# A Fourier filter and a gated layer in one kernel: the order and the padding of the constant tiles

## The chip, the cores and the metric

One core of one Trainium2 chip runs the whole program. The metric is device time in microseconds of that core. The kernel before was timed in three runs; the profile is one more, profiled, execution.

## The reference

Two steps follow each other. The first filters each of 8 sequences (3008 steps, 256 channels) in the frequency domain; the second sends the 24064 resulting tokens through a layer 256 to 2048 to 256 with a rational function between.

```python
X = np.fft.rfft(x, axis=1)
Y = X * (filt_r + 1j * filt_i)[None, :, :]
x2 = np.fft.irfft(Y, n=x.shape[1], axis=1).reshape(B * S, D)

h = x2 @ w_in
P = a[0] + a[1] * h + a[2] * h * h + a[3] * h ** 3
Q = 1.0 + abs(b[0]) * abs(h) + abs(b[1]) * h * h
out = (P / (Q + 1e-06)) @ w_out
```

## The kernel before

The Fourier transform of 3008 = 64 x 47 points is done as matrix products, in fp32. Stage 1 (L290) multiplies the input `xin` by the matrix `a1_sb`, a view of `small_sb` (L298), and sends the result through a scratch buffer in HBM (`scr`). Stage 2 multiplies by the first of three 128 x 128 matrices in `mats_sb` (L346), by the filter with signs from `sgn_sb` (L331, L353, L354, L365), by the second or third matrix (L379, L381), and stores to a second scratch buffer. Stage 3 (L408) multiplies tiles `tl` of that buffer by `e_sb`, the other view of `small_sb` (L424), and splits the result into a high and a low part, `xh` and `xl`, in the type fp32r.

The layer then runs in 752 units: 47 tiles of 512 tokens, 16 slices of 128 hidden rows each. A unit makes six matmuls of 128 x 128 by 128 x 512 from `wi_sb` and `xh`, `xl` into a PSUM bank (L457, L458, L460). ScalarE forms squares, an absolute value and a reciprocal root of it (L465 to L487), GpSimd a scaled term and a product (L497, L516), VectorE the numerator and the high and low part of the result, `hi` and `lo` (L502, L511, L519, L525). Six more matmuls with `wo_sb` add into two output banks (L534 to L536). The scalars of these steps are columns of `cf_sb`, computed once at the start from `ab_sb` and `abs_sb` by some 50 small steps (L138 to L187), and four of them are loaded into registers of ScalarE (L190).

The weights come as 64-bit numbers; 16 pieces are decoded into `wi_sb` and `wo_sb` (high and low parts, L210 to L246), 12 of them while batch 0 is transformed. Batches 1 to 7 are transformed in between the units. TensorE, ScalarE, VectorE and GpSimd run in the order in which the program is written; the DMA queue of SyncE does so in the head, and is ordered by the planner afterwards.

All tiles in SBUF come from pools that are laid out one behind the other: constants (L114 to L125, in this order: small_sb, mats_sb, sgn_sb, ab_sb, wi_sb, wo_sb, abs_sb, cf_sb, flag_sb), then `conv`, `mlp` and `x`. Each tile takes its bytes per partition, rounded up to 32. The first byte of the constants is 16512 = 129 x 128.

Of the kernel before, what the change touches and what calls it, by code (L numbers as in the profile page):

```python
# [9 lines left out]
F32 = mybir.dt.float32  # L10
F32R = mybir.dt.float32r
I32 = mybir.dt.int32
# [13 lines left out]
K2 = 24  # L26
R1 = 96
C = 256
G = 94
DFF = 2048  # L30
LAG = 4
RATES = 0.6, 0.38
# [26 lines left out]
def shape_constants():  # L59
    n2 = np.arange(N2)  # L60
    k2 = np.arange(K2)
    th = 2 * np.pi * np.outer(n2, k2) / N2
    a1 = np.zeros((48, 2, K2, 2, 2))
    for h in range(2):
        a1[:N2, h, :, 0, h] = np.cos(th)
        a1[:N2, h, :, 1, h] = -np.sin(th)
    a1 = a1.reshape(R1, R1)

    ph = 2 * np.pi * np.outer(np.arange(N1), np.arange(N1)) / N1
    co, si = np.cos(ph), np.sin(ph)  # L70
    fwd = np.block([[co, -si], [si, co]])
    inv = np.block([[co, si], [-si, co]])

    e = np.zeros((K2, 2, 2, 2, N2))
    w = np.where(k2 == 0, 1.0, 2.0) / S
    for h in range(2):
        e[:, 0, h, h, :] = w[:, None] * np.cos(th.T)
        e[:, 1, h, h, :] = -w[:, None] * np.sin(th.T)
    e = e.reshape(R1, G)

    k = (N2 * np.arange(N1)[:, None] + N1 * k2[None, :]) % S
    sgn = np.where(k > S // 2, -1.0, 1.0)
    sgn[(k == 0) | (k == S // 2)] = 0.0
    sgn = np.concatenate([sgn, -sgn], 0)
    mats = np.zeros((128, 3, 128))
    mats[:, 0], mats[:, 1], mats[:, 2] = fwd, inv, np.concatenate([inv[64:], inv[:64]])
    small = np.zeros((R1, R1 + G))
    small[:, :R1], small[:, R1:] = a1, e
    f = lambda v: np.ascontiguousarray(v, dtype=np.float32)
    return f(mats), f(small), f(sgn)  # L90

# [10 lines left out]
def conv_moe(ctx: ExitStack, tc: tile.TileContext, xp, fr, fi, w_in, w_out, ab, mats, small, sgn, outT):  # L102
# [3 lines left out]
    consts = ctx.enter_context(tc.tile_pool(name="consts", bufs=1))  # L106
# [4 lines left out]
    ps = ctx.enter_context(tc.tile_pool(name="ps", bufs=1, space=PSUM))  # L111
    pso = ctx.enter_context(tc.tile_pool(name="pso", bufs=1, space=PSUM))

    small_sb = consts.tile([R1, R1 + G], F32, name="small_sb")  # L114
    a1_sb, e_sb = small_sb[:, :R1], small_sb[:, R1:]
    mats_sb = consts.tile([128, 3, 128], F32, name="mats_sb")
    sgn_sb = consts.tile([128, K2], F32, name="sgn_sb")
    ab_sb = consts.tile([128, 12], F32, name="ab_sb")

    wi_sb = consts.tile([128, 4, 2, 2, TT], F32R, name="wi_sb")  # L120
    wo_sb = consts.tile([128, 8, 2, TT], F32R, name="wo_sb")
    xh = xl = None
    abs_sb = consts.tile([128, 12], F32, name="abs_sb")
    cf_sb = consts.tile([128, 24], F32, name="cf_sb")
    flag_sb = consts.tile([128, 1], I32, name="flag_sb")  # L125

    v = nc.vector
    ts, tt, stt = v.tensor_scalar, v.tensor_tensor, v.scalar_tensor_tensor
# [279 lines left out]
    def stage3(k):  # L408
# [11 lines left out]
        for cc in range(2):  # L420
            yield 1.1
            bank, pt = banks.tile(f"x_{k}_{cc}")
            for i in range(g1 - g0):
                nc.tensor.matmul(  # L424
                    pt[:, i * G : i * G + G], tl[:, i, cc * 128 : cc * 128 + 128], e_sb, start=True, stop=True
                )
            yield

            t0, t1 = g0 * G, g1 * G
            cut = min(t1, (t0 // RX + 1) * RX)  # L430
# [129 lines left out]
    def run(gen):  # L560
        for _ in gen:
            pass
# [85 lines left out]
    def pipeline(squares):  # L648
# [10 lines left out]
        for i in range(n + LAG + 2 * OG):  # L659
# [14 lines left out]
            if i < 16:  # L674
# [4 lines left out]
                while dec.done < i // 4 * 4 + 3:  # L679
                    dec.load()  # L680
                    dec.step()
            if f == 0 and xgen and T * (t + 1) > chunks[xk - 1][0] * G:
                run(xgen)
# [134 lines left out]
```

## Time and profile before

| | us |
|---|---|
| median of 3 runs | 2585.64 (2584.13 to 2586.91) |
| the profiled execution | 2588.73 |
| its span, from first to last instruction | 2586.1 |

| engine | busy us | share |
|---|---|---|
| PE (matmul) | 2526.4 | 98% |
| DVE (VectorE) | 2269.5 | 88% |
| ACT (ScalarE) | 2198.9 | 85% |
| POOL (GpSimd) | 1856.3 | 72% |

PE is the time in which a matmul was under way; neighbouring matmuls overlap, so their mean durations add up to more than the span. PEld is the loading of weights, which runs beside the matmuls. The mean granted clock of TensorE was 0.989 of full speed. In the rows, L12 is line 12 of the kernel.

### The profile page before, as it was taken

How to read it: one execution, taken by the hardware profiler on the slowest of the kernel's cores; microseconds unless marked ns; L12 is line 12 of the kernel's file. 1: busy time of each engine (PE TensorE's matmuls, PEld its weight loads, DVE VectorE, ACT ScalarE, POOL GpSimd, SP SyncE). 2: the span in 40 equal slices, each digit the busy share in tenths (PEclk: the TensorE clock that was granted, in tenths of full speed). 3: DMA queues.
4: the chain of work that ended last, by engine and by line, in shares of the span. 5: the costliest groups of instructions: out<-in, count | busy, mean ns of one | idle time of the engine just before them, and what ended most of it. 6: DMA issues, size and time to landing. Idle time of an engine off the chain costs nothing.

```text
span 2586.1 us, 35887 instructions
## 1 busy us (share of the span) xinstructions
PE 2526.4 (98%) x10712; PEld 1936.0 (75%) x10712; DVE 2269.5 (88%) x3549; ACT 2198.9 (85%) x4170; POOL 1856.3 (72%) x1984
## 2 busy tenths in 40 slices
PE   4799999999999999999999999999999999999998
PEld 1467777777777777777777777777777778888886
DVE  5689988999889998899888998899988999899998
ACT  4588889888988889888888889888888889999997
POOL 3468876788668876778657886688757787677676
PEclk8799999999999999999999999999999999999999
DMA  8653331332223231232223332233323210000000
GB/s 248 181 139 104 100 113 51 107 93 86 71 75 100 81 95 53 84 109 83 74 61 105 86 93 71 67 101 88 87 61 94 82 37 28 25 25 17 25 9 18
DMA packets 102813, 208.76 MB, mean 81 GB/s; under 512 B 8752, under 2 KB 58512, under 8 KB 102608
## 3 DMA queue, kind: packets, MB, share of 16 engines
q1 hardware_dynamic: 99568, 199.79, 26.5%
q10 hardware_dynamic: 3040, 6.58, 1.0%
q8 instruction: 87, 1.43, 0.2%
q14 instruction: 118, 0.97, 0.1%
HBM read 131.36 MB, written 74.97 MB: 80 GB/s over the span
## 4 chain that ended last, share of the span: by engine, by line
PE 95%; DVE 2%; DMA 2%; ACT 1%; issue 0%; ACTq 0%; SPq 0%; DVEq 0%
PE o L534 13%; PE o L535 13%; PE o L536 13%; PE h_u L458 13%; PE h_u L460 13%; PE h_u L457 13%; PE x L424 4%; PE s L298 4%; PE y L346 3%; PE z L379 3%; DMA scr<-s1e 1%; DMA xin<-xp 0%; ACT s1e L263 0%; DMA ab_sb<-ab 0%; DVE hi_u L511 0%
## 5 line engine op out<-in xcount | busy, mean ns | idle before, releaser
L516 POOL TENSOR_TENSOR q_u<-q_u,hi_u 128x512 f32<-128x512 f32 x752 | 974.6, 1296 | 526.8 <-DVE hi_u L511 509.3
L534 PE MATMUL o<-hi_u,wo_sb 128*128 128x512 f32 x1504 | 705.6, 469 | 0.0
L465 ACT ACTIVATE q_u<-h_u 128x512 f32<-128x512 f32 x752 | 450.5, 599 | 243.3 <-PE h_u L460 175.2
L511 DVE SCALAR_TENSOR_TENSOR hi_u<-h_u,cf_sb,a_u 128x512 fp32r<-128x512 f32 x752 | 559.9, 745 | 76.4 <-ACT a_u L487 68.0
L519 DVE SCALAR_TENSOR_TENSOR h_u<-h_u,cf_sb,q_u 128x512 f32<-128x512 f32 x752 | 565.4, 752 | 54.1 <-POOL q_u L516 53.7
L457 PE MATMUL h_u<-xh,wi_sb 128*128 128x512 f32 x1504 | 604.3, 402 | 3.1 <-DVE xl L435 1.9
L458 PE MATMUL h_u<-xl,wi_sb 128*128 128x512 f32 x1504 | 596.9, 397 | 0.0
L535 PE MATMUL o<-lo_u,wo_sb 128*128 128x512 f32 x1504 | 594.3, 395 | 1.4 <-DVE lo_u L525 1.4
L536 PE MATMUL o<-hi_u,wo_sb 128*128 128x512 f32 x1504 | 594.2, 395 | 0.0
L497 POOL TENSOR_SCALAR q_u<-q_u,cf_sb 128x512 f32<-128x512 f32 x752 | 584.0, 777 | 3.6 <-ACT a_u L482 3.6
L502 DVE SCALAR_TENSOR_TENSOR h_u<-w_u,cf_sb,h_u 128x512 f32<-128x512 f32 x752 | 561.5, 747 | 4.3 <-ACT w_u L472 4.3
L525 DVE TENSOR_TENSOR lo_u<-h_u,a_u 128x512 fp32r<-128x512 f32 x752 | 514.3, 684 | 0.1
L482 ACT ACTIVATE a_u<-q_u 128x512 f32<-128x512 f32 x752 | 475.3, 632 | 0.1
L460 PE MATMUL h_u<-xh,wi_sb 128*128 128x512 f32 x1504 | 473.8, 396 | 0.0
L487 ACT ACTIVATE a_u<-a_u 128x512 f32<-128x512 f32 x752 | 470.3, 625 | 0.0
L478 ACT ACTIVATE q_u<-q_u 128x512 f32<-128x512 f32 x752 | 469.4, 624 | 0.0
L472 ACT ACTIVATE w_u<-h_u 128x512 f32<-128x512 f32 x752 | 443.9, 590 | 0.0
L534 PEld LDWEIGHTS o<-hi_u,wo_sb 128*128 128x128 f32 x1504 | 282.8, 188 | 117.2 <-issue 63.3
L535 PEld LDWEIGHTS o<-lo_u,wo_sb 128*128 128x128 f32 x1504 | 283.0, 188 | 116.7 <-issue 60.3
L457 PEld LDWEIGHTS h_u<-xh,wi_sb 128*128 128x128 f32 x1504 | 283.4, 188 | 77.9 <-issue 3.6
L458 PEld LDWEIGHTS h_u<-xl,wi_sb 128*128 128x128 f32 x1504 | 283.5, 188 | 73.2 <-issue 4.4
L460 PEld LDWEIGHTS h_u<-xh,wi_sb 128*128 128x128 f32 x1504 | 283.6, 189 | 69.1
(96 smaller groups left out, 1888.9 us busy)
## 6 DMA issues: line engine op xcount, KB each, us to landing
xin<-xp SPq DMA_DIRECT2D x64, 384.0 KB, 3.8
scr<-s1e SPq DMA_DIRECT2D x64, 384.0 KB, 4.1
xin<-scr SPq DMA_DIRECT2D x48, 512.0 KB, 4.9
scr<-ev SPq DMA_DIRECT2D x48, 512.0 KB, 4.8
outT<-oe SPq DMA_DIRECT2D x47, 512.0 KB, 3.1
f<-fr SPq DMA_DIRECT2D x87, 256.0 KB, 4.1
f<-fi SPq DMA_DIRECT2D x87, 256.0 KB, 3.9
tl<-scr SPq DMA_DIRECT2D x44, 480.0 KB, 4.0
```

The source lines that it names most:

```text
L457: nc.tensor.matmul(o, w_in_part(0, f, cc), xh[:, cc, ts], start=cc == 0, stop=False)
L458: nc.tensor.matmul(o, w_in_part(0, f, cc), xl[:, cc, ts], start=False, stop=False)
L460: nc.tensor.matmul(o, w_in_part(1, f, cc), xh[:, cc, ts], start=False, stop=cc == 1)
L497: nc.gpsimd.tensor_scalar(out=self.q, in0=self.q, scalar1=AIK, scalar2=SGN, op0=ALU.mult, op1=ALU.add)
L502: v.scalar_tensor_tensor(out=H, in0=w, scalar=PK, in1=H, op0=ALU.add, op1=ALU.mult)
L511: nc.vector.scalar_tensor_tensor(out=self.hi, in0=self.H, scalar=self.p0, in1=self.a, op0=ALU.add, op1=ALU.mult)
L516: nc.gpsimd.tensor_tensor(out=self.q, in0=self.q, in1=self.hi.bitcast(F32), op=ALU.mult)
L519: nc.vector.scalar_tensor_tensor(out=self.H, in0=self.H, scalar=self.p0, in1=self.q, op0=ALU.add, op1=ALU.subtract)
L525: nc.vector.tensor_tensor(out=self.lo, in0=self.H, in1=self.a, op=ALU.mult)
L534: nc.tensor.matmul(o, w_out_part(0, f, dd), self.hi, start=f == 0, stop=False)
L535: nc.tensor.matmul(o, w_out_part(0, f, dd), self.lo, start=False, stop=False)
L536: nc.tensor.matmul(o, w_out_part(1, f, dd), self.hi, start=False, stop=f == 15)
```

## The change

The constants are allocated in another order and with other sizes. `wi_sb` and `wo_sb` come first, then `mats_sb`, then `small_sb`, whose second matrix gets 96 columns in place of 94 (the last two zero; `e_sb` is still 94 columns wide). The five small constants become columns of one tile `words` of 128 words: `sgn_sb` from column 0, `ab_sb` from 32, `abs_sb` from 64, `cf_sb` from 96, and the flag in column 120. No instruction is added or taken away; the array `small` that the program is given is 96 x 192 and not 96 x 190.

```diff
+GE = 96
...
-    small = np.zeros((R1, R1 + G))
-    small[:, :R1], small[:, R1:] = a1, e
+    small = np.zeros((R1, R1 + GE))
+    small[:, :R1], small[:, R1 : R1 + G] = a1, e
...
-    small_sb = consts.tile([R1, R1 + G], F32, name="small_sb")
-    a1_sb, e_sb = small_sb[:, :R1], small_sb[:, R1:]
-    mats_sb = consts.tile([128, 3, 128], F32, name="mats_sb")
-    sgn_sb = consts.tile([128, K2], F32, name="sgn_sb")
-    ab_sb = consts.tile([128, 12], F32, name="ab_sb")
...
     wi_sb = consts.tile([128, 4, 2, 2, TT], F32R, name="wi_sb")
     wo_sb = consts.tile([128, 8, 2, TT], F32R, name="wo_sb")
     xh = xl = None
-    abs_sb = consts.tile([128, 12], F32, name="abs_sb")
-    cf_sb = consts.tile([128, 24], F32, name="cf_sb")
-    flag_sb = consts.tile([128, 1], I32, name="flag_sb")
+    mats_sb = consts.tile([128, 3, 128], F32, name="mats_sb")
+    small_sb = consts.tile([R1, R1 + GE], F32, name="small_sb")
+    a1_sb, e_sb = small_sb[:, :R1], small_sb[:, R1 : R1 + G]
+    words = consts.tile([128, 128], F32, name="words_sb")
+    sgn_sb, ab_sb, abs_sb, cf_sb = words[:, :K2], words[:, 32:44], words[:, 64:76], words[:, 96:120]
+    flag_sb = words[:, 120:121].bitcast(I32)
```

## Rows read from the trace of the kernel before

**Rows 1.** The page: span, busy us and share, the chain's share by engine.
```profile
span 2586.1 us, 35887 instructions
...
PE 2526.4 (98%) x10712; PEld 1936.0 (75%) x10712; DVE 2269.5 (88%) x3549; ACT 2198.9 (85%) x4170; POOL 1856.3 (72%) x1984
...
PE 95%; DVE 2%; DMA 2%; ACT 1%; issue 0%; ACTq 0%; SPq 0%; DVEq 0%
```

**Rows 2.** The page's groups: line, count | busy us, mean ns | idle before; one of six.
```profile
L460 PE MATMUL h_u<-xh,wi_sb 128*128 128x512 f32 x1504 | 473.8, 396 | 0.0
```

**Rows 3.** Timeline of PE in the tail: start us, us, line; twelve steps apart.
```profile
2570.98 0.39 PE L534 MATMUL o<-hi_u,wo_sb 128*128 128x512 f32 x1
...
2573.78 0.39 PE L534 MATMUL o<-hi_u,wo_sb 128*128 128x512 f32 x1
```

**Rows 4.** Windows: length, busy us (count) by engine, PEclk, DMA share, GB/s.
```profile
101.00:106.00 5.00, 5.00 (x12) 3.60 (x12) 0.97 (x3) 2.38 (x7) 2.56 (x2) 0.50 1.00 266
2470.00:2570.00 100.00, 100.00 (x430) 80.17 (x429) 97.08 (x149) 94.81 (x182) 73.93 (x73) 1.00 0.03 11
0.00:105.00 105.00, 62.58 (x136) 27.99 (x137) 63.21 (x134) 44.12 (x71) 41.73 (x52) 0.83 0.83 237
```

**Rows 5.** The chain in order of time, steady stretch: start us, us, what.
```profile
1035.55 0.86 PE s L298 x2
1039.20 1.09 PE x L424 x10
```

**Rows 6.** Timeline of PE in the head, first units: start us, us, line.
```profile
102.64 0.63 PE L457 MATMUL h_u<-xh,wi_sb 128*128 128x512 f32 x1
103.07 0.63 PE L458 MATMUL h_u<-xl,wi_sb 128*128 128x512 f32 x1
```

**Rows 7.** Tiles mats_sb and wi_sb, weight loads: ns min/median/max, first and last start.
```profile
L346 PEld LDWEIGHTS y<-xin,mats_sb x192: 186/188/337, 52.3 to 2123.5; 128*128 128x128 f32 x192
...
L457 PEld LDWEIGHTS h_u<-xh,wi_sb x1504: 186/188/338, 101.3 to 2568.4; 128*128 128x128 f32 x188
```

**Rows 8.** Groups of the first 200 us, decoding on DVE: busy us, mean ns.
```profile
L234 DVE SCALAR_TENSOR_TENSOR dp<-raw,dp 128x512 int32<-128x512 int32 x16 | 11.1, 696 | 0.6
...
L238 DVE SCALAR_TENSOR_TENSOR dq<-raw,dp 128x512 f32<-128x512 uint32 x12 | 8.2, 686 | 0.4
```

**Rows 9.** Timeline of DVE in a steady unit: start us, us, line.
```profile
1500.28 0.68 DVE L525 TENSOR_TENSOR lo_u<-h_u,a_u 128x512 fp32r<-128x512 f32 x1
...
1502.85 0.68 DVE L525 TENSOR_TENSOR lo_u<-h_u,a_u 128x512 fp32r<-128x512 f32 x1
```

**Rows 10.** The chain in order of time, head: start us, us, what.
```profile
0.73 5.24 DMA ab_sb<-ab
...
6.84 1.28 ACT L138
...
15.54 0.23 DVE cf_sb L187
...
16.15 2.05 ACT s1e L263 x4
...
100.96 9.91 DMA xin<-xp
```

**Rows 11.** DMA issues by line: queue, count, KB each, us to landing.
```profile
xin<-scr SPq DMA_DIRECT2D x48, 512.0 KB, 4.9
...
outT<-oe SPq DMA_DIRECT2D x47, 512.0 KB, 3.1
...
small_sb<-small ACTq DMA_DIRECT2D x1, 71.2 KB, 7.0
```

**Rows 12.** Tiles sgn_sb and cf_sb: ns min/median/max, first to last start us; landing us.
```profile
L615 ACTq DMA_DIRECT2D sgn_sb<-sgn x1: 444/444/444, 6.4 to 6.4; - x1
...
DMA to landing us min/median/max: 8.3/8.3/8.3
...
L190 ACTq TENSOR_LOAD <-cf_sb x4: 275/281/473, 12.3 to 15.8; - x4
```

## The prediction

> **What bounds the kernel now.** I read the page from the top: the span, the busy line and the chain. PE is busy 98% of 2586.1 us, 95% of the chain that ended last runs through it, and nothing else has more than 2% of the chain [rows 1]. The groups of the page say what PE does: six lines (L457, L458, L460, L534 to L536) with 1504 matmuls each, 9024 in all, on fp32r operands of 512 columns [rows 2]. Their mean durations overlap, so they are no price. The price is the spacing of starts. In the tail, twelve steps on PE from 2570.98 take 2.80 us, 233.3 ns each [rows 3]. A window of 100 us ahead of it holds 430 matmuls, 232.6 ns each, at clock 1.00 with PE busy throughout [rows 4]. So 9024 x 233.3 ns = 2105 us of the span is this one stream. The convolution's fp32 passes come from the chain in order of time: two L298 passes take 0.86 us (430 ns each), ten L424 pieces 1.09 us (109 ns each) [rows 5]. By the loops, with each product in two passes, there are 256 of L298, 192 of L346, 216 of L379 and L381, and 1024 of L424; taken at these prices that is (256 + 192 + 216) x 0.430 + 1024 x 0.109 = 397 us. Together 2502 of 2586 us; the other 84 us lie in the head, the first 105 us, where PE is busy 62.58 us, the clock is 0.83 and the DMA share 0.83 [rows 4].
>
> One thing in these rows matters for a change of addresses. A 430 ns pass is two sweeps of 512 columns, 215 ns each. The fp32r matmul has one sweep and takes 233.3 ns: an excess of 18.3 ns that is there 9024 times, 165 us in all. [...]
>
> **The change part by part.** No instruction is added or taken away, no wait is written, no queue is reordered. What moves is addresses. The allocator rounds each tile up to 32 bytes, and the constants begin at byte 16512, 129 x 128. Before: small_sb 768, mats_sb 1536, sgn_sb 96 and ab_sb 64 bytes put wi_sb and wo_sb at 32 past a multiple of 128; abs_sb, cf_sb and flag_sb (64 + 96 + 32) put every tile of the pools behind (xin, ev, filters, tl, oe, a, w, q, hi, lo, xh, xl) at 96 past one. small_sb and mats_sb were at 0. After: 32768 + 32768 + 1536 + 768 + 512 bytes, all at 0, and the pools move up by 160 bytes.
>
> Weights, 32 to 0: the trace has weight loads from both places. L346 loads from mats_sb (at 0), median 188 ns; L457 from wi_sb (at 32), median 188 ns [rows 7]. Price 0, and the load is not what PE waits for, since it fits in each 233 ns.
>
> Moving operands, 96 to 0: no row shows an fp32r stream from a start at 0, so I bound it. The nearest rows are the 430 ns passes of L298, whose moving operand xin also lay at 96 and which run without the excess [rows 5]; that speaks against the address. The lower end is the excess gone, 9024 x 18.3 = -165 us. The upper end: weights and moving operand were 64 bytes apart modulo 128 and now start alike; if their reads get in each other's way by 1 ns more per matmul, that is +9 us. I take 0, by the row of L298. [...]
>
> VectorE, ScalarE, GpSimd: the same 512 elements, written to PSUM (L234, 696 ns) or to a tile at 96 (L238, 686 ns), cost the same on VectorE [rows 8]. Price 0; if a few ns went, PE would hide it, for VectorE needs 2.57 us per unit of four such steps (1500.28 to 1502.85) [rows 9] and PE 12 x 233.3 = 2.80. The cover is 0.23 us per unit: it also says what is late next if PE got faster.
>
> DMA: the rows of 4096 bytes in SBUF start at other addresses. On the chain this counts in the head alone; its DMA pieces in the chain are 5.24, 6.02, 4.61, 9.61, 6.15, 3.85, 3.17, 2.34 and 9.91 us, together 51 us (first and longest in [rows 10]). Even a tenth of it, either way, would be 5 us; I take 0, as the same 512 KB lands in 3.1 us from oe and 4.9 us into xin, both at 96: the load on the engines sets it, not the place [rows 11]. small_sb grows from 71.2 to 72 KB, 1% of a landing of 7.0 us, 0.1 us.
>
> Scalars: sgn, ab, abs, cf and the flag now share one tile. Columns, engines and order stay; price 0 as long as the waits stay by columns (rival 2).
>
> Sum: 0 + 0 + 0 + 0.1 against the profiled 2588.7 us (span 2586.1 and 2.6 around it). The median of the runs shown is 3.1 us lower, 2585.6; I forecast 2585.
>
> **The rivals.** 1: the start address is what holds the fp32r stream. For it: the excess is the same 18.3 ns in all six lines, and all of them have the same addresses modulo 128. Against it: the fp32 passes from 96, and weight loads that don't care. Whole: 2585.6 - 165 = 2421; VectorE with 2.57 us per unit would then lie just under PE with 12 x 215 = 2.58, so some of it would go back. In part: each ns of the 18.3 is 9.0 us; three ns give 2559. [...]
>
> 2: slower, by the shared tile. If waits are held per tile and not per column, the first ScalarE step (L138, at 6.84 [rows 10]) and all small VectorE steps behind it wait for the sign table, issued at 6.4 and landed 8.3 us later, at 14.7 [rows 12]. Then the chain of small steps that ends with L187 at 15.54 and lets the first evacuation start at 16.15 comes 7.8 us later [rows 10], with stage 1 queued behind it on ScalarE: 2585.6 + 7.8 = 2593. It decides from 5.2 us on. Against it: ScalarE's first register load from cf_sb starts at 12.3, while VectorE still writes other columns of cf_sb until 15.54 [rows 10, 12]. So the wait goes by columns, not by the tile.
>
> 3: slower, by reads of weights and moving operand that now begin alike, as priced above: from 0.6 ns per matmul on it would show, 1 ns gives 2595. Nothing in the trace speaks for it.
>
> **How the numbers follow.** A measurement of this kernel can tell 0.2%, 5.2 us. No change: 0.62. Rival 1 whole 0.08, in part 0.16; rival 2 0.05; rival 3 0.09. So faster 0.24, same 0.62, slower 0.14. The range from 2556 to 2598 holds the first, about two thirds of the partial gains (up to 3.3 ns per matmul), rival 2, and rival 3 up to 1.4 ns; whole recovery is left out.
>
> **What would show it.** In the changed kernel: the spacing of matmul starts in the tail, 233.3 ns again or less, decides between the forecast and rivals 1 and 3; in the matmul-only window the count of 430 in 100 us says the same. Weight loads at 188 ns and L238 at 686 ns would show that the other readers and writers don't care. L138 at 6.8 us and the first evacuation at 16.2 us show that the shared tile adds no wait. The forecast is wrong if the spacing moves by over 0.6 ns, or if the first unit's matmul starts over 5 us from 101.3 [rows 7].

## The result

The changed kernel takes 2542.89 us (median of 4 runs, 2542.57 to 2545.82) against 2586.27 us for the kernel before (median of 4 runs): a ratio of 0.9833, 95% interval 0.9816 to 0.9850, 43 us less. The prediction, 2585 us and no change, was wrong, and the time lies 13 us under the range.

The page of the changed kernel, the lines that answer to [rows 1]: span, busy us and share, the chain's share by engine.

```profile
span 2543.2 us, 35887 instructions
...
PE 2479.4 (97%) x10712; PEld 1934.2 (76%) x10712; DVE 2264.1 (89%) x3549; ACT 2197.0 (86%) x4170; POOL 1850.8 (73%) x1984
...
PE 93%; DVE 2%; DMA 2%; ACT 1%; issue 0%; SPq 0%; ACTq 0%; DVEq 0%
```

The same instructions in the same number; nearly all of the busy time that went is PE's, 47 us; VectorE, ScalarE and GpSimd lost 6 us or less each. The timeline of PE in the tail, beside [rows 3], shows how (start us, us, line; twelve steps from the first to the last):

```profile
2528.14 0.39 PE L534 MATMUL o<-hi_u,wo_sb 128*128 128x512 f32 x1
2528.37 0.39 PE L535 MATMUL o<-lo_u,wo_sb 128*128 128x512 f32 x1
...
2530.86 0.39 PE L534 MATMUL o<-hi_u,wo_sb 128*128 128x512 f32 x1
```

2.72 us for twelve steps are 226.7 ns each, where it was 233.3. Over the whole layer after 200 us, the mean of the differences between neighbouring matmul starts (those over 260 ns, where PE does something else between, left out) fell from 233.3 to 228.1 ns. Over all 9024 matmuls that is 9024 x 5.2 = 47 us. In this profiled execution the first unit starts 5 us later than in [rows 7] (106.4 against 101.3 us), which leaves 42 us, and the span fell by 42.9. A second profiled execution of the changed kernel (after_again, below) starts its first unit at 102.5 us, so the later start is not shown to come from the change.

Windows of the changed kernel (length, busy us (count) for PE, PEld, DVE, ACT and POOL, granted clock, DMA share, GB/s), beside [rows 4]:

```profile
2430.00:2530.00 100.00, 100.00 (x443) 82.85 (x442) 99.15 (x153) 97.51 (x187) 75.98 (x75) 1.00 0.03 11
0.00:105.00 105.00, 59.30 (x123) 25.23 (x124) 62.35 (x131) 42.22 (x66) 39.04 (x50) 0.82 0.81 228
```

The window holds 443 matmuls in 100 us where there were 430, at the same granted clock of 1.00. The head has nearly the same clock (0.82, it was 0.83) and DMA share (0.81, it was 0.83); PE has done less in it (59.30 us, it was 62.58), as the first unit comes later. VectorE, busy 97.08 us of 100 before, is now at 99.15: it keeps up, barely.

The other operations kept their prices. The tiles wi_sb and mats_sb (weight loads, ns min/median/max, first and last start), beside [rows 7]:

```profile
L457 PEld LDWEIGHTS h_u<-xh,wi_sb x1504: 186/188/338, 106.4 to 2525.7; 128*128 128x128 f32 x188
```
```profile
L346 PEld LDWEIGHTS y<-xin,mats_sb x192: 186/188/338, 53.3 to 2092.2; 128*128 128x128 f32 x192
```

Groups of the first 200 us on VectorE (busy us, mean ns), beside [rows 8]:

```profile
L234 DVE SCALAR_TENSOR_TENSOR dp<-raw,dp 128x512 int32<-128x512 int32 x16 | 11.2, 697 | 0.6
...
L238 DVE SCALAR_TENSOR_TENSOR dq<-raw,dp 128x512 f32<-128x512 uint32 x12 | 8.2, 686 | 0.4
```

And the chain in the head, beside [rows 10], with the register loads from the shared tile, beside [rows 12]:

```profile
6.43 1.28 ACT L138
```
```profile
L190 ACTq TENSOR_LOAD <-words_sb x4: 280/283/473, 11.9 to 15.4; - x4
```

L138 starts as early as before and the register loads run from 11.9 to 15.4 us: the shared tile adds no wait.

### The profile page after: what moved, and what is told of

Read it like the earlier page. It is cut to its first block, busy times and chain, and to the rows that moved or that the text cites. A ratio compares the mean times of both kernels' runs of the same rounds, so it can differ in the third digit from the quotient of the medians.

```text
span 2543.2 us, 35887 instructions
## 1 busy us (share of the span) xinstructions
PE 2479.4 (97%) x10712; PEld 1934.2 (76%) x10712; DVE 2264.1 (89%) x3549; ACT 2197.0 (86%) x4170; POOL 1850.8 (73%) x1984
## 4 chain that ended last, share of the span: by engine, by line
PE 93%; DVE 2%; DMA 2%; ACT 1%; issue 0%; SPq 0%; ACTq 0%; DVEq 0%
PE o L534 13%; PE o L535 13%; PE o L536 13%; PE h_u L458 13%; PE h_u L457 13%; PE h_u L460 13%; PE x L424 4%; PE s L298 4%; PE y L346 3%; PE z L379 3%; DMA scr<-s1e 1%; DMA fxl<-fi 0%; DVE hi_u L511 0%; DVE h_u L519 0%; ACT q_u L478 0%
## 5 line engine op out<-in xcount | busy, mean ns | idle before, releaser
L511 DVE SCALAR_TENSOR_TENSOR hi_u<-h_u,words_sb,a_u 128x512 fp32r<-128x512 f32 x752 | 561.7, 747 | 60.3 <-ACT a_u L487 57.6
L519 DVE SCALAR_TENSOR_TENSOR h_u<-h_u,words_sb,q_u 128x512 f32<-128x512 f32 x752 | 567.1, 754 | 52.4 <-POOL q_u L516 52.1
L457 PE MATMUL h_u<-xh,wi_sb 128*128 128x512 f32 x1504 | 596.3, 396 | 5.4 <-DVE xl L435 4.0
L458 PE MATMUL h_u<-xl,wi_sb 128*128 128x512 f32 x1504 | 588.2, 391 | 0.0
L497 POOL TENSOR_SCALAR q_u<-q_u,words_sb 128x512 f32<-128x512 f32 x752 | 579.3, 770 | 3.5 <-ACT a_u L482 3.5
L502 DVE SCALAR_TENSOR_TENSOR h_u<-w_u,words_sb,h_u 128x512 f32<-128x512 f32 x752 | 563.3, 749 | 4.2 <-ACT w_u L472 4.2
L460 PE MATMUL h_u<-xh,wi_sb 128*128 128x512 f32 x1504 | 464.6, 390 | 0.0
L534 PEld LDWEIGHTS o<-hi_u,wo_sb 128*128 128x128 f32 x1504 | 283.2, 188 | 112.2 <-issue 63.3
L457 PEld LDWEIGHTS h_u<-xh,wi_sb 128*128 128x128 f32 x1504 | 283.0, 188 | 73.6 <-DVE lo_u L525 4.3
L536 PEld LDWEIGHTS o<-hi_u,wo_sb 128*128 128x128 f32 x1504 | 282.5, 188 | 61.8
```

Of the source, the lines that this page charges most:

```text
L457: nc.tensor.matmul(o, w_in_part(0, f, cc), xh[:, cc, ts], start=cc == 0, stop=False)
L458: nc.tensor.matmul(o, w_in_part(0, f, cc), xl[:, cc, ts], start=False, stop=False)
L460: nc.tensor.matmul(o, w_in_part(1, f, cc), xh[:, cc, ts], start=False, stop=cc == 1)
L497: nc.gpsimd.tensor_scalar(out=self.q, in0=self.q, scalar1=AIK, scalar2=SGN, op0=ALU.mult, op1=ALU.add)
L502: v.scalar_tensor_tensor(out=H, in0=w, scalar=PK, in1=H, op0=ALU.add, op1=ALU.mult)
L511: nc.vector.scalar_tensor_tensor(out=self.hi, in0=self.H, scalar=self.p0, in1=self.a, op0=ALU.add, op1=ALU.mult)
```

## The experiments

In what follows, *distance* is the byte at which the weights start less the byte at which the moving operands start, modulo 256, worked out from the layout that each program was built with. The kernel before has 32 - 224, a distance of 64; the changed kernel has 128 - 128, a distance of 0. *Mean* is the mean spacing of starts as defined above, over the layer after 200 us. Two starts are *alike* where the distance is 0.

### The addresses alone, and each half of them

The kernel before with unused tiles put in. Addresses alone (e_pads):

```diff
     ab_sb = consts.tile([128, 12], F32, name="ab_sb")
+    pad0 = consts.tile([128, 24], F32, name="pad0")
...
     flag_sb = consts.tile([128, 1], I32, name="flag_sb")
+    pad1 = consts.tile([128, 16], F32, name="pad1")
```

> The kernel before with its constants in their old order and five small tiles, and two unused tiles of 96 and 64 bytes put in, so that the weights and all pools start at a multiple of 128 as in the changed kernel. If the addresses alone are the cause: matmul spacing 226.7 ns and about 2543 us. If the shared tile of the small constants has a part: it stays near 2586 us, or between.

Measured: 2543.06 us, ratio 0.9832 (0.9816 to 0.9849), mean 228.1 ns. The tail (nine steps, 2.04 us, 226.7 ns each):

```profile
2526.28 0.39 PE L536 MATMUL o<-hi_u,wo_sb 128*128 128x512 f32 x1
...
2528.32 0.40 PE L536 MATMUL o<-hi_u,wo_sb 128*128 128x512 f32 x1
```

So the gain comes from the addresses; the order of the constants, the padded matrix and the shared tile have no part in it.

Weights alone at a multiple of 128 (e_wonly: `pad0` of 24 words, `pad1` of 8):

> The kernel before, with 96 bytes ahead of the weights and 32 behind them: weights start at a multiple of 128, all pools (the moving operands xh, xl, hi, lo among them) stay at 96 past one. If the start of the moving operand is the cause: 233.3 ns and 2586 us. If the start of the weights is: 226.7 ns and 2543 us. If each has a half: 230 ns and about 2565 us.

Moving operands alone (e_ponly: `pad1` of 8 words, no `pad0`):

> The kernel before, with 32 bytes behind the flag: the pools (moving operands) start at a multiple of 128, the weights stay at 32 past one. If the start of the moving operand is the cause: 226.7 ns and 2543 us. If the start of the weights is: 233.3 ns and 2586 us. If each has a half: 230 ns and about 2565 us.

Measured: 2585.55 us (ratio 0.9996, 0.9986 to 1.0005; mean 233.2 ns) and 2586.38 us (1.0000, 0.9991 to 1.0010; 233.1 ns). The tails of the two, nine steps each, 2.10 and 2.11 us:

```profile
2568.57 0.40 PE L536 MATMUL o<-hi_u,wo_sb 128*128 128x512 f32 x1
...
2570.67 0.40 PE L536 MATMUL o<-hi_u,wo_sb 128*128 128x512 f32 x1
```
```profile
2568.35 0.40 PE L535 MATMUL o<-hi_u,wo_sb 128*128 128x512 f32 x1
...
2570.46 0.40 PE L535 MATMUL o<-hi_u,wo_sb 128*128 128x512 f32 x1
```

Neither half brings anything. No theory written down before these runs said that: a cost of the moving operand's start, one of the weights' start and a half of each all fall. Either both must lie on a line, or what counts is how the two lie to each other.

The table (t1_table) spread the starts within one kernel: eight chunks per weight matrix, nine slots of hi and lo, xh and xl, each at a residue of its own.

```diff
...
-            return mlp.tile([128, TT], dt, tag=f"{tag}{self.i % RING[tag]}", name=f"{tag}_u{self.i}")
+            wide = TT + 8 * (tag in ("hi", "lo"))
+            tile_ = mlp.tile([128, wide], dt, tag=f"{tag}{self.i % RING[tag]}", name=f"{tag}_u{self.i}")
+            return tile_[:, :TT]
...
```

> The changed kernel with the starts spread on purpose: eight chunks of either weight matrix at 0, 32, 64, 96, 0, ... past a multiple of 128, the five hi slots at 0, 32, 96, 32, 96, the four lo slots at 64, 0, 64, 0, xh at 32, xl at 96. If the moving operand's start decides, the spacing after a hi matmul goes by its slot (226.7 ns at 0, 233.3 at 32 and 96) and doesn't go by the chunk; if the weights' start decides, it goes by the chunk alone; at 64 the lo slots tell whether 64 bytes are enough (226.7) or 128 are needed (233.3).

Measured: 2576.97 us (one run), mean 232.0 ns. Sorted by slot and by chunk (pairs of neighbours within one product) the means lie between 230.4 and 232.8 ns with no clear order: neither the slot nor the chunk decides. No slot and no chunk comes near 226.7 ns, whatever its own place. This table was the wrong design; the kernels below hold one distance throughout.

### On a line, or alike

The kernel before with pads, so that both begin at 64 past a multiple of 128 (e_64_64: 8 and 16 words), both at 32 past one (e_32_32: 16 words behind the flag alone), or weights at 0 and moving operands at 64 (e_w0_m64: 24 words ahead of the weights alone). And the changed kernel with both at multiples of 512 (e_512: 96 and 64 words).

> The kernel before with unused tiles so that the weights and all pools start at 64 past a multiple of 128. Theory of 64: reads go by lines of 64 bytes and both streams must start on one: 226.7 ns and 2543 us. Theory of 128: 233.3 ns and 2586 us. Theory of likeness (both streams at the same place modulo 128): 226.7 ns and 2543 us.

> The same with weights and all pools at 32 past a multiple of 128. Theory of 64: off the line, 233.3 ns and 2586 us. Theory of 128: 233.3 ns and 2586 us. Theory of likeness: 226.7 ns and 2543 us.

> The same with the weights at 0 and all pools at 64 past a multiple of 128. Theory of 64: 226.7 ns and 2543 us. Theory of 128: 233.3 ns and 2586 us. Theory of likeness: 233.3 ns and 2586 us.

> The changed kernel with 384 unused bytes ahead of the weights and 256 behind the small constants: weights and pools at multiples of 512, where the changed kernel has them at 128 and 384 past one. If 64 or 128 is all that counts: 226.7 ns and 2543 us as the changed kernel. If larger lines count too: the spacing falls again by some ns towards 215, each ns being 9 us as long as VectorE and ScalarE follow.

Measured: 2539.64 us (0.9818, 0.9799 to 0.9838; mean 228.0 ns), 2539.91 us (0.9819, 0.9800 to 0.9839; 227.5), 2588.50 us (1.0007, 0.9997 to 1.0017; 233.3) and 2543.19 us (0.9833, 0.9817 to 0.9850; 228.1). The tails of e_32_32 (six steps, 1.36 us) and of e_w0_m64 (twelve steps, 2.80 us):

```profile
2522.16 0.39 PE L535 MATMUL o<-hi_u,wo_sb 128*128 128x512 f32 x1
...
2523.52 0.39 PE L535 MATMUL o<-hi_u,wo_sb 128*128 128x512 f32 x1
```
```profile
2570.35 0.39 PE L535 MATMUL o<-hi_u,wo_sb 128*128 128x512 f32 x1
...
2573.15 0.39 PE L535 MATMUL o<-hi_u,wo_sb 128*128 128x512 f32 x1
```

226.7 ns with nothing on a multiple of 64, and 233.3 ns with both on one. So lines of 64 and of 128 bytes fall, and likeness stands. A coarser multiple, 512, brings no more: the changed kernel has weights and moving operands 256 apart modulo 512, e_512 has them alike.

Side by side, to see whether the place still counts where both are alike (the kernel of e_32_32 again, and the changed kernel again, five rounds each):

> The kernel before with unused tiles, weights and pools alike at 32 past a multiple of 128, against the changed kernel on the same chip. If the place itself counts: about 2540 us, some 3 us under the changed kernel. If only the likeness counts: within 1 us of it.

> The changed kernel again, for comparison: 2543 us and 226.7 ns by either theory; within 1 us of the kernel alike at 32 if the place doesn't count.

Measured: 2543.30 us (2537.24 to 2543.62) and 2543.50 us (2541.16 to 2545.52). The means of the spacing were 227.5 and 228.1 ns again, which would be 9024 x 0.6 = 5 us; the medians don't separate, with the first unit at 104.9 us in the one profiled execution and at 102.5 in the other. By the times, the place makes no difference that could be shown, and no version beats the changed kernel beyond doubt.

### Alike modulo what, and how nearly

The changed kernel with 32 words behind the small constants, all tiles still at multiples of 128, but weights at 128 and pools at 0 modulo 256 (e_r128):

```diff
     flag_sb = words[:, 120:121].bitcast(I32)
+    pad1 = consts.tile([128, 32], F32, name="pad1")
```

> The changed kernel with 128 unused bytes behind the small constants: weights at 128 and pools at 0 modulo 256, all multiples of 128 still. Likeness modulo 128: 226.7 ns and 2543 us. Likeness modulo 256: 233.3 ns and 2586 us.

Measured: 2580.60 us, ratio 0.9972 (0.9958 to 0.9986), mean 232.6 ns. The tail (twelve steps, 2.81 us):

```profile
2561.80 0.40 PE L535 MATMUL o<-hi_u,wo_sb 128*128 128x512 f32 x1
...
2564.61 0.40 PE L535 MATMUL o<-hi_u,wo_sb 128*128 128x512 f32 x1
```

Every tile lies at a multiple of 128 bytes here, and nearly all of the gain is gone. It takes likeness modulo 256. That the changed kernel has it follows from where its tiles happen to end: weights and pools both at 128 past a multiple of 256.

A second table (t2_table: the eight chunks of wo_sb 16 bytes apart modulo 128, the quarters of wi_sb at distances 0, 4, 128 and 256) was meant to give the curve in one run:

> The changed kernel with all moving operands at one place and the eight chunks of wo_sb at distances of 0, 16, 32, ... 112 bytes from it modulo 128 (at 128 plus these modulo 256); the four quarters of wi_sb at distances 0, 4, 128 and 256. If likeness modulo 128 is the rule and all or nothing: 226.7 ns for chunk 0 of wo and quarters 0, 2, 3 of wi, 233.3 ns for the rest. If likeness modulo 256 is: chunk 0 of wo and quarter 2 of wi are at 233.3. If the cost grows with the distance: a staircase between. If another distance than 0 is better still: some chunk lies under 226.7.

Measured: 2567.68 us (one run), mean 231.1 ns. Taken as in the first table, the quarters of wi_sb at distances 0 and 256 came out at 229.6 and 228.1 ns, those at 4 and 128 at 232.4 and 232.6: the order is that of likeness modulo 256, but blurred. The chunks of wo_sb lie at distances of 128 to 240, none of them alike, and came out between 228.3 and 233.3 ns in no order of distance. So single distances in kernels of their own: weights 32 ahead of the moving operands (e_neg32: `pad1` of 8 words), and both weight matrices shifted by one word or four:

```diff
-    wi_sb = consts.tile([128, 4, 2, 2, TT], F32R, name="wi_sb")
-    wo_sb = consts.tile([128, 8, 2, TT], F32R, name="wo_sb")
+    wi_all = consts.tile([128, 8192 + 64], F32R, name="wi_sb")
+    wo_all = consts.tile([128, 8192 + 64], F32R, name="wo_sb")
+    wi_sb = wi_all[:, 4 : 8192 + 4].rearrange("p (a b c d) -> p a b c d", a=4, b=2, c=2)
+    wo_sb = wo_all[:, 4 : 8192 + 4].rearrange("p (a b c) -> p a b c", a=8, b=2)
```

> The changed kernel with 32 unused bytes behind the small constants: the weights lie 32 ahead of the moving operands modulo 256, where all slow kernels so far have them 32, 64 or 128 past. If only likeness modulo 256 is fast: 233.3 ns and 2586 us. If a distance of some bytes in this direction is as good or better: 226.7 ns or less and 2543 us or less.

> The changed kernel with both weight matrices 4 bytes past the place that is like their moving operands modulo 256. If equal starts are needed to the word: 233.3 ns and 2586 us. If only the 32 or 16 bytes count in which both begin: 226.7 ns and 2543 us.

> The changed kernel with both weight matrices 16 bytes past the place that is like their moving operands modulo 256. If equal starts are needed within 16 bytes: 233.3 ns and 2586 us. If a piece of 32 bytes or more is what counts: 226.7 ns and 2543 us.

Measured, with the kernels that hold one distance throughout (the diff is that of e_rel16; e_rel4 shifts by 1 word in place of 4; medians from several chips, whose kernel before takes 2586.27 to 2588.03 us):

| distance, bytes | kernel | us | mean ns |
|---|---|---|---|
| 0 | changed; e_pads; e_512 | 2542.89; 2543.06; 2543.19 | 228.1; 228.1; 228.1 |
| 0 | e_64_64; e_32_32 | 2539.64; 2539.91 | 228.0; 227.5 |
| 4 | e_rel4 | 2578.89 | 232.4 |
| 16 | e_rel16 | 2566.55 | 230.9 |
| 32 | e_wonly; e_ponly | 2585.55; 2586.38 | 233.2; 233.1 |
| 64 | before; e_w0_m64 | 2586.27; 2588.50 | 233.3; 233.3 |
| 128 | e_r128 | 2580.60 | 232.6 |
| -32 | e_neg32 | 2584.36 | 233.0 |

Of these distances only 0 gives the whole gain; those between 128 and 224 were not held by any kernel throughout. Four bytes are enough to lose most of the gain, and at 16 about half is left (two runs). That half is an average over time: by stretches of 100 us the spacing of e_rel16 changes between some 227.5 and 232.5 ns, and from 2200 us on, where of the convolution only pieces of stage 3 are left, it stays at 233.3. Its tail (six steps, 1.40 us):

```profile
2523.01 0.40 PE L536 MATMUL o<-hi_u,wo_sb 128*128 128x512 f32 x1
...
2524.41 0.40 PE L459 MATMUL h_u<-xh,wi_sb 128*128 128x512 f32 x1
```

So at a given distance the stream can run at either pace. Where the pace changes, the timeline shows (four steps of the stream in 0.93 us, a convolution pass, four steps in 0.90 us):

```profile
236.16 0.39 PE L538 MATMUL o<-hi_u,wo_sb 128*128 128x512 f32 x1
...
237.09 0.40 PE L460 MATMUL h_u<-xl,wi_sb 128*128 128x512 f32 x1
...
237.79 1.02 PE L381 MATMUL z<-f,mats_sb 128*128 128x512 f32 x2
...
238.88 0.39 PE L537 MATMUL o<-lo_u,wo_sb 128*128 128x512 f32 x1
...
239.78 0.39 PE L538 MATMUL o<-hi_u,wo_sb 128*128 128x512 f32 x1
```

The convolution's fp32 matmuls cut the stream of e_rel16 into 347 stretches of eight or more steps behind 200 us. The mean of 139 of them lies between 226.6 and 228.0 ns, that of the other 208 between 232.0 and 234.1, and of none between these: the pace is picked when the stream starts again behind fp32 matmuls, and kept to the next ones. What picks it stays open.

The changed kernel shows the same starts in another way. Behind an fp32 pass its first two steps take 233.3 and 232.5 ns on average, the next six 228.6 to 232.4, and from the ninth on each takes 226.7.

### One of the two products alike

The changed kernel with 16 words between wi_sb and wo_sb and 48 behind the small constants: the products into h at distance 0, those into o at 64 (e_half).

> The changed kernel with 64 unused bytes between the two weight matrices and 192 behind the small constants: wi_sb and its moving operands lie alike modulo 256, wo_sb lies 64 past its moving operands. If the relation of weights and moving operand decides matmul by matmul: 226.7 ns for the six matmuls into h, 233.3 for the six into o, about 2565 us. If it takes only one stream out of step for the whole kernel: 233.3 ns for all, 2586 us. If it is not this relation but the place of the pools alone: 226.7 ns for all, 2543 us.

Measured: 2577.19 us, ratio 0.9967 (0.9948 to 0.9987); means 231.1 ns into h and 233.1 into o. Four steps into h (0.93 us) and six into o (1.40 us) in the tail:

```profile
2555.88 0.39 PE L459 MATMUL h_u<-xh,wi_sb 128*128 128x512 f32 x1
...
2556.81 0.62 PE L462 MATMUL h_u<-xh,wi_sb 128*128 128x512 f32 x2
2557.27 0.39 PE L536 MATMUL o<-hi_u,wo_sb 128*128 128x512 f32 x1
...
2558.67 0.40 PE L536 MATMUL o<-hi_u,wo_sb 128*128 128x512 f32 x1
```

Half of the matmuls alike bring under a quarter of the gain, not half: the six good ones between six bad ones stay at 231.1 ns, which fits the up to eight steps that the changed kernel needs for it. That may also be why both tables came out blurred.

### Is it time that the next weights take?

The weight loads run beside the matmuls (PEld busy 76% of the span of the changed kernel, PE 97%). At granted clock 0.50 [rows 4] the kernel before starts its fp32r matmuls 427 ns apart, 3.42 us for the eight steps from the first line of [rows 6] to this one of the same timeline:

```profile
106.06 0.79 PE L460 MATMUL h_u<-xh,wi_sb 128*128 128x512 f32 x2
```

The 17 spacings at that clock in its head are 426.6 ns on average. Half of that, 213.3 ns, is my estimate of what the 512 columns take at the full clock. The 13.4 and 20 ns by which 226.7 and 233.3 lie over it could be what the reading of the next weights takes away. These kernels load 64 weight columns in place of 128 for two of three matmuls into o (corrections left out for half of the output rows).

```diff
-                nc.tensor.matmul(o, w_out_part(0, f, dd), self.lo, start=False, stop=False)
-                nc.tensor.matmul(o, w_out_part(1, f, dd), self.hi, start=False, stop=f == 15)
+                n = 64 if f < 15 else 128
+                nc.tensor.matmul(o[:n], w_out_part(0, f, dd)[:, :n], self.lo, start=False, stop=False)
+                nc.tensor.matmul(o[:n], w_out_part(1, f, dd)[:, :n], self.hi, start=False, stop=f == 15)
```

> The changed kernel; the second and third matmul of each product into o (lo with the high weights, hi with the low ones) use 64 of 128 weight columns except in the last slice, so these corrections are left out for half of the output rows. The moving operands stay 512 columns. If the 13.4 ns over 213.3 are what the next weights' reading takes from the moving stream, in proportion to its bytes: about 220 ns while 64 columns are loaded, 226.7 while 128 are. If they are a fixed cost per matmul: 226.7 ns everywhere.

> The kernel before with the same corrections left out for half of the output rows. In proportion to the bytes of the next weights: about 223.3 ns while 64 columns are loaded, 233.3 while 128 are. A fixed cost per matmul: 233.3 ns everywhere. A fixed part by the address and one by the bytes: 226.7 ns against 233.3.

Measured: 2551.20 us for the changed kernel with half-width loads (e_cols_like) and 2585.03 us for the kernel before with them (e_cols_unlike), one run each; means into o 229.1 and 232.6 ns, where the full kernels have 228.8 and 233.3. The groups of weight loads of the second from 2300 to 2500 us (mean ns) and its tail, three steps in 0.70 us:

```profile
L534 PEld LDWEIGHTS o<-hi_u,wo_sb 128*128 128x128 f32 x138 | 26.0, 188 | 9.1
...
L536 PEld LDWEIGHTS o<-lo_u,wo_sb 128*64 128x64 f32 (+1 forms) x138 | 19.1, 139 | 5.9
```
```profile
2563.05 0.40 PE L534 MATMUL o<-hi_u,wo_sb 128*128 128x512 f32 x1
2563.29 0.39 PE L536 MATMUL o<-lo_u,wo_sb 128*64 128x512 f32 x1
2563.52 0.39 PE L537 MATMUL o<-hi_u,wo_sb 128*64 128x512 f32 x1
2563.75 0.40 PE L534 MATMUL o<-hi_u,wo_sb 128*128 128x512 f32 x1
```

The loads got shorter (139 ns on average with the full ones of the last slice, against 188), the spacing hardly (232.6 against 233.3). A cost in proportion to the bytes of the next weights falls: it asked for 220 and 223 ns. Where the operands are alike, the shorter loads even did harm: from 2200 us on the mean of e_cols_like is 229.2 ns against 227.0 in the changed kernel, and the run takes 8 us more. So a distance of 0 alone doesn't give 226.7 ns. The relation of the two streams decides, but not as time taken byte for byte; the mechanism stays open.

## Why the prediction was wrong

**What bounds the kernel** stood: the 9024 fp32r matmuls and their spacing, the excess of 18.3 ns over 215, half of a 430 ns pass [rows 5], and that each nanosecond is worth 9 us. At granted clock 0.50 a pass took 0.855 us (below), again twice the 0.427 of an fp32r matmul. The whole gain lies in that term: 47 us of spacing, of which the profiled execution gave 5 back in its head. Of the 84 us that the sum left to the head, PE's idle time there explains 105 - 62.58 = 42.4 us [rows 4]; the forecast didn't rest on the rest.

**Weights, 32 to 0: price 0.** The loads take 188 ns at either place, as said. But the duration of a load, 188 ns in both kernels, says nothing on the spacing of the stream beside it, 233.3 ns in the one and 226.7 in the other.

**Moving operands, 96 to 0: "I take 0, by the row of L298".** This is the step that failed, twice. First the row: a pass of L298 takes 430 ns for 512 columns, about half the pace of the fp32r stream; it has weights at 0 and a moving operand at 96 modulo 128, and I saw no excess in it. I read this as "the start doesn't matter". In the head of the kernel before, at granted clock 0.50, two passes of L298 take 1.71 us, 0.855 each (start us, us, line):

```profile
24.42 1.06 PE L298 MATMUL s<-xin,small_sb 96*96 96x512 f32 x1
...
26.13 1.06 PE L298 MATMUL s<-xin,small_sb 96*96 96x512 f32 x1
```

So 430 ns at the full clock is half of that to 3 ns, where the fp32r stream lies 20 ns over half of its 426.6. The row only shows that a stream at half the pace has no such cost; it is silent on the fast one. (The fp32 passes of L379 keep their 428 ns in the changed kernel, too.) The lesson was in the same paragraph: no row had an fp32r stream at another address. Then the thing varied: I priced each operand by its own start. e_wonly and e_ponly show that moving either start alone brings nothing, and the table that the distance of the two modulo 256 counts: at 0 the excess shrinks by 5.2 ns on average, 9024 x 5.2 = 47 us, where I had put 0.

**The upper end of that step (rival 3)** named the right relation, weights and moving operands that begin alike, with the wrong sign: I let it cost 1 ns, it gains 5.2. It was based on nothing but a picture of two readers in each other's way. It also worked the starts out modulo 128 alone; that the changed layout is alike modulo 256 was not foreseen.

**Rival 1, in part,** is the forecast that came nearest: each nanosecond 9.0 us, and 5.2 of the 18.3 came back. Its mechanism, the start address of the moving operand, fell all the same. Its reason, that all six lines have the same addresses modulo 128, was sound: all six also had the same distance. And the range held only 3.3 ns of it, a cut that had no row behind it.

**Rival 2,** the shared tile: no wait, L138 at 6.43 and the register loads from 11.9 to 15.4 us, as argued from the columns; e_pads shows the same time without it.

**VectorE late next:** 2.57 us per unit against 12 x 226.7 = 2.72 leaves 0.15 us, out of which the evacuations of the output banks have to come as well, and 99.15 us of 100 are busy. That the mean is 228.1 ns and not 226.7 costs 9024 x 1.4 = 13 us. It is lost while the convolution runs (227.9 to 228.8 ns by stretches of 100 us from 200 to 2100 us, 226.9 to 227.1 behind). It goes to the starts of the stream behind fp32 matmuls, not to VectorE: from the ninth step of a stretch on the spacing is 226.7 ns, with the convolution running and without.

**The other prices** held: L238 686 ns, L234 697. The head's DMA pieces did not stay as they were: 11.87 us of `fxl<-fi` stand on the chain of the changed kernel, and the first unit's matmul at 106.4 us is 5.1 from 101.3, which the prediction also named as a sign of being wrong. The second profiled execution has 9.37 us there and 102.5, so this is not shown to be an effect of the change.

## What to carry to other kernels

Where PE is the bound with a stream of fp32r matmuls, look at the spacing of starts against half of the spacing at granted clock 0.50 (213.3 ns here), and try a layout with the weights and all moving operands at the same place modulo 256 bytes (shown here for 128 x 128 by 128 x 512 alone); a pad among the constants is all it takes (64 bytes in e_32_32), and any small tile put in later can undo it (32 bytes in e_neg32: 2584.36 us). Keep the alike matmuls in long unbroken stretches, for here the first eight steps behind fp32 matmuls took 228.6 to 233.3 ns, the later ones 226.7. Check the layout by addresses, not by the name of a rule: "all at multiples of 128" lost nearly everything again with 128 bytes more. And a price of zero read from a row of another mode, at another pace, is no bound: without a row of the same stream at another value, its whole excess belongs into the range.

## What the runs showed of the hardware

At the full granted clock the mean spacing of 128 x 128 by 128 x 512 fp32r matmuls over the layer was 233.0 to 233.3 ns at distances of 32, 64 and -32 bytes between weights and moving operand, 232.6 ns at 128, 232.4 at 4, 230.9 at 16, and 227.5 to 228.1 at 0. In unbroken stretches of the tail it was 233.3 ns in the kernel before and 226.7 in the changed one. At granted clock 0.50 it was 426.6 ns in the kernel before; 226.7 and 233.3 lie 13.4 and 20 ns over half of that. An fp32 pass of L298 took 0.855 us at granted clock 0.50 and 0.430 at 1.00. The pace belongs to the stream, not to the single matmul: with only half of the matmuls at distance 0, under a quarter of the gain was left (10 of 43 us), and at 16 bytes the same kernel runs at both paces in turn (226.6 to 228.0 and 232.0 to 234.1 ns), one for each stretch between fp32 matmuls. At distance 0 the stream needs up to eight steps behind fp32 matmuls (228.6 to 233.3 ns) to reach 226.7 ns. Half-width weight loads shortened the load (139 ns on average against 188) and not the spacing (232.6 ns into o against 233.3); at distance 0 they raised it from 227.0 to 229.2 ns in the tail.
